# A list schedule's model of VectorE, GpSimd and TensorE: when one holds the other, how long GpSimd takes, how early TensorE may be planned

## The chip, the cores and the metric

One core of one Trainium2 chip runs the whole program. The metric is device microseconds of one execution. The kernel before takes 1219.08 us (median of three runs, 1217.67 to 1220.74).

Names in the profile: PE is TensorE (its weight loads are PEld), DVE is VectorE, ACT is ScalarE, POOL is GpSimd, SP is the engine that issues the DMAs.

## The reference

Attention with queries averaged in pairs, then a gated feed-forward block that mixes along the sequence. There are 8 batches and 8 heads; 1152 keys and 576 queries of width 64.

```python
q_pool = q.reshape(B, H, S // 2, 2, D).mean(axis=3)
scores = scale * np.matmul(q_pool, k.transpose(0, 1, 3, 2))
scores = scores - np.max(scores, axis=-1, keepdims=True)
attn = np.exp(scores)
attn = attn / (np.sum(attn, axis=-1, keepdims=True) + 1e-09)
x = np.matmul(attn, v)              # laid out as (8, 576, 512)
...
h = np.maximum(x @ w_in, 0.0)
u, v = (h[..., :d_ff // 2], h[..., d_ff // 2:])
v_n = (v - mu) / np.sqrt(var + 1e-06)
v_s = np.einsum('ts,bsd->btd', w_spatial, v_n) + b_spatial[None, :, None]
out = (u * v_s) @ w_out
```

All of it is kept near float32 by splitting each float32 operand into a float16 head and a float16 rest and multiplying the parts.

## The kernel before, in words

**Attention.** The two heads of a pair lie on the two halves of the partitions, so there are 32 pairs, `i` = 0 to 31. For each pair, `prep` squares, scales and splits the queries and keys (the part that VectorE does in the first eight pairs, by `rest`, L387, GpSimd does later, L605), and issues DMAs on SP that bring the parts into place. `maxima` multiplies queries and keys roughly (L641, tiles `pm` and `pw`: 27 products of 128x384 a pair), VectorE takes the largest of each product (L647, `mt`), and `shift` makes a row of it (L660 to L670), turned by TensorE (L668). While `units` holds a gated unit, `maxima` takes all its tiles from the two banks of `pm`; without one it alternates between these and the two of `pw`. `attention` then makes the exact scores in 18 steps of two matmuls (L842, L843, tile `pss`), ScalarE takes the exponent (L848, tile `pt`, eight buffers), GpSimd subtracts the upper half of each float32 from it and so leaves a float16 rest (L868, 128x512), and `values` multiplies with V in three groups of four matmuls: two on the upper halves (L745, L751), which need ScalarE alone, and one on the rests (L756), which needs GpSimd too. What is left over of the queries (64 of each head) goes through `ptl` in the same manner, with one GpSimd instruction of 128x1152 for each pair.

**The gated part.** Two batches make a unit, four units in all. `gated_unit` multiplies with w_in (L926, L990), normalises (L962 to L974 on VectorE and ScalarE), mixes along the sequence (L1031, L1032), gates (L1038, L1041), splits (L387, tile `vv`) and multiplies with w_out (L1074). Units 0 to 2 are fed in small pieces between the steps of attention; the last one runs behind the attention.

**What sets the order.** The program is written down once in the order of these generators. Then `Order.pin` makes a list schedule: it has a cost for each instruction (`cost`: how long the engine is taken, and when the result is there), keeps the time at which each engine is free, and again and again takes the earliest instruction that may start on any engine; on one engine the one that was written first goes first among those that are due. What it takes is chained to the engine's instruction before it, so the order on every engine is the plan's order, and on the chip only semaphores decide when each starts. An instruction is due when its producers are through, plus `DELAY`, plus `SLACK` for its pair of engines: with `("Pool", "PE")` at 2100 ns, a matmul that reads what GpSimd made is not due until 2.1 us after the planned end of that. The slack bears on the choice alone; the planned start of what is chosen leaves it out (`there`, not `due`).

`two_from_sbuf` marks instructions that may hold each other up: on VectorE tensor by tensor, tensor by scalar and copy with no operand in PSUM, and on GpSimd all of its tensor subtractions and additions. For these the plan keeps `held`, the start and end of the last planned GpSimd instruction, and `dve`, when the last such VectorE instruction lets GpSimd go:

```python
if e == "DVE":
    if t >= held[0]:
        t = max(t, held[1] - 130)
    dve = t + out
else:
    t = max(t, dve)
    held = (t, t + out)
```

So in the plan a VectorE instruction that starts at or after the start of a GpSimd one begins 130 ns before the end of it at the soonest, and a GpSimd instruction begins when the VectorE one has ended.

Of the kernel before, what the change touches and what calls it, by code (L numbers as in the profile page):

```python
# [10 lines left out]
F16 = mybir.dt.float16  # L11
BF16 = mybir.dt.bfloat16
F32 = mybir.dt.float32
# [18 lines left out]
class Order:  # L32

    LANES = ("PE", "Activation", "DVE", "Pool", "SP")
    DELAY = {("PE", "Activation"): 114, ("Activation", "Pool"): 77}
    SLACK = {("Pool", "PE"): 2100, ("Activation", "PE"): 300, ("DVE", "PE"): 300, ("SP", "PE"): 500}
    SIZE = {F16: 2, BF16: 2, F32: 4, I32: 4, U32: 4, I64: 8}

    def __init__(self):
# [106 lines left out]
    def cost(self, lane, ins):  # L148

        xs = [x.bass_ap for x in list(ins.ins) + list(ins.outs) if hasattr(x, "bass_ap")]  # L150
        count = lambda ap: math.prod([d[1] for d in ap.ap][1:])
        if lane == "PE":
            n = count(xs[0])
            t = max(28.5, n / 2.4 + 2.5)
            if xs[0].dtype == F32:
                t = 110 if n == 128 else max(224, 4 * n / 2.4)
            return t, t + 148
        if lane == "SP":
            big = max((count(x) * x.ap[0][1] * self.SIZE[x.dtype] for x in xs), default=0)
            return (1230 if "Transpose" in ins.opcode else 560), 2400 + big / (100 if "Transpose" in ins.opcode else 230)  # L160
        n = max((count(x) for x in xs), default=1)
        psum = any(self.slot.get(x.tensor.name, (0, 0))[1] for x in xs)

        flat = sum(count(x) == 1 for x in xs[:-1]) if n > 1 else 0
        wide = len(xs) - 1 - flat
        if lane == "Activation":
            t = 0.84 * n + (157 if psum else 188) + 85 * (min(flat, 2) or (n == 1 and wide > 1))
            if len(ins.outs) > 1:
                return t - 10, t + 95
            return t - 105, t  # L170
        elif lane == "DVE":
            plain = ins.opcode == "TensorScalarPtr"
            if plain and wide < 2 and not psum or ins.opcode == "TensorCopy":
                t = 0.55 * n + 140 + 60 * flat
            else:
                t = 1.04 * n + 145 + 65 * (flat > 0 and plain)
        else:
            t = {F32: 2.1, F16: 2.0, BF16: 1.74}[xs[1].dtype] * n + 150
            return t - 42, t
        return t - 84, t  # L180

# [5 lines left out]
    def pin(self, tc):  # L187
        names = {getattr(mybir.EngineType, e): e for e in self.LANES}
        fixed = ("RegisterMove", "TensorScalarAffineSelect", "Memset")
        prog = [i for i in tc.nc.cur_bb.bb.instructions if i.engine in names and i.opcode not in fixed]  # L190
        before, begun = self.edges(prog)
        loose = {i.name for a, z, skip in self.lined if skip for i in tc.nc.cur_bb.bb.instructions[a:z]}
        early = {i.name for i in tc.nc.cur_bb.bb.instructions[: self.seen]} - loose
        ahead = None
        for n, i in enumerate(prog):
            if names[i.engine] == "SP" and i.name not in loose:
                if ahead is not None and ahead not in before[n]:
                    begun[n].add(ahead)
                if i.name in early:
                    ahead = n  # L200
        after = [[] for _ in prog]
        left = []
        lane = [names[i.engine] for i in prog]
        for n, (pre, beg) in enumerate(zip(before, begun)):
            left.append(len(pre) + len(beg))
            for m in pre:
                after[m].append((n, True))
            for m in beg:
                after[m].append((n, False))
        cost = [self.cost(e, i) for e, i in zip(lane, prog)]  # L210
        shared = [e in ("DVE", "Pool") and self.two_from_sbuf(i) for e, i in zip(lane, prog)]
        held, dve = (0.0, 0.0), 0.0
        ready = {e: [n for n in range(len(prog)) if lane[n] == e and not left[n]] for e in self.LANES}
        due = [0.0] * len(prog)
        there = [0.0] * len(prog)
        free = dict.fromkeys(self.LANES, 0.0)
        wire = 0.0
        load = {n for n, i in enumerate(prog) if lane[n] == "SP" and i.ins and i.ins[0].bass_ap.tensor.name not in self.slot}
        last = {}
        dep = mybir.DependencyInfo(mybir.DependencyClass.NoSync, mybir.DependencyReason.DATA)  # L220
        for _ in prog:
            best = None
            for e, ns in ready.items():
                if ns:

                    at = {n: max(due[n], wire - 1000) if n in load else due[n] for n in ns}
                    if e == "DVE":
                        for n in ns:
                            if shared[n] and max(free[e], at[n]) >= held[0]:
                                at[n] = max(at[n], held[1] - 130)  # L230
                    t = max(free[e], min(at.values()))
                    n = min(n for n in ns if at[n] <= t)
                    if best is None or t < best[0]:
                        best = (t, e, n)
            t, e, n = best
            ready[e].remove(n)
            own, out = cost[n]
            t = max(free[e], there[n])
            if shared[n]:

                if e == "DVE":
                    if t >= held[0]:
                        t = max(t, held[1] - 130)
                    dve = t + out
                else:
                    t = max(t, dve)
                    held = (t, t + out)
            if e == "SP":
                wire = max(wire, t + own) + (out - 2400)
                end = wire + 1700  # L250
            else:
                end = t + out
            free[e] = t + own
            if e in last:
                tc.add_manual_dep(prog[n], last[e], dep, reason="order")
            last[e] = prog[n].name
            for m, through in after[n]:
                left[m] -= 1
                if not through:
                    x = t  # L260
                elif lane[m] != e:
                    x = end + self.DELAY.get((e, lane[m]), 52)
                else:
                    x = t if e == "PE" else end + 34
                there[m] = max(there[m], x)
                due[m] = max(due[m], x + (self.SLACK.get((e, lane[m]), 0) if through else 0))
                if not left[m]:
                    ready[lane[m]].append(m)
        self.span = max(free.values())
# [964 lines left out]
```

## Time and profile before

| | before |
|---|---|
| median of 3 runs | 1219.08 us |
| the profiled execution | 1220.91 us |
| its span in the trace | 1219.1 us |
| granted TensorE clock, mean | 0.987 |
| ACT busy | 890.8 us (73%) |
| HBM read, written | 81.20 MB, 9.44 MB |

The span is what the trace covers of the program's instructions; 1.8 us of the execution lie outside it. A view by windows gives, for each stretch of the span, how long each engine was busy in it and how many instructions that were. A view of waits tells which instruction's idle time was ended by which. In a timeline, a row is the start, the length, engine, line, operation, the tile written and the tiles read, and the shape; where equal instructions follow one another, they are merged and counted, and what stands in brackets is the engine's idle time before the row, and what ended it.

### The profile page before, as it was taken

Reading aid. Unit: us, or ns where it says so; the run is one execution under the profiler, and the core shown is the slowest. Engines: PE = TensorE matmul, PEld = TensorE weight load, DVE = VectorE, ACT = ScalarE, POOL = GpSimd, SP = SyncE. Lnnn points to the kernel's source line nnn. Section 1 sums busy time; section 2 is a strip of 40 time slices with the busy share of each in tenths; the row PEclk is TensorE's granted clock in tenths of the full one; section 3 lists DMA queues with packets and bytes.
Section 4 is the critical chain, followed back from the end, with each engine's and each line's share of the span. In section 5 each row is a group of like instructions: output and inputs, shape, how many; then the busy total and the mean of one; then the engine's idle time right before and its main releaser. Section 6 shows DMA issues by size and latency. Waiting matters only on the chain.

```text
span 1219.1 us, 33464 instructions
## 1 busy us (share of the span) xinstructions
PE 1160.2 (95%) x13296; PEld 726.5 (60%) x13296; DVE 887.9 (73%) x2228; ACT 890.8 (73%) x1675; POOL 841.1 (69%) x726
## 2 busy tenths in 40 slices
PE   3988999999998999999999999999999999999998
PEld 1656666766655666566665666566665666655453
DVE  5699989987889577766679676865669866841644
ACT  4887779789976877978777877878776876744433
POOL 2545657678886878888887887788887786874000
PEclk9889999999999999999999999999999999999999
DMA  5455455445432454255442443256334421211002
GB/s 190 163 156 161 123 178 143 125 119 153 130 87 77 138 123 123 73 158 152 114 101 75 125 140 82 65 143 204 99 98 103 103 70 49 48 47 45 1 1 79
DMA packets 88446, 132.97 MB, mean 109 GB/s; under 512 B 39840, under 2 KB 48032, under 8 KB 87776
## 3 DMA queue, kind: packets, MB, share of 16 engines
q1 hardware_dynamic: 88288, 130.82, 38.4%
q8 instruction: 104, 1.70, 0.6%
q14 instruction: 54, 0.44, 0.1%
HBM read 81.20 MB, written 9.44 MB: 74 GB/s over the span
## 4 chain that ended last, share of the span: by engine, by line
PE 71%; DVE 22%; issue 2%; ACT 1%; DMA 1%; POOL 0%; SPq 0%; DVEq 0%; ACTq 0%
DVE mt L647 8%; PE pss L842 7%; PE pss L843 7%; PE pm L641 7%; PE pw L1031 7%; PE pw L926 6%; PE pw L1074 5%; PE pw L990 5%; PE o L745 4%; PE o L756 4%; PE o L751 4%; DVE vv L387 2%; PE o L738 1%; DVE row L962 1%; PE pss L926 1%
## 5 line engine op out<-in xcount | busy, mean ns | idle before, releaser
L868 POOL TENSOR_TENSOR pt<-pt 128x512 f16<-128x512 f32 x528 | 574.1, 1103 | 195.8 <-ACT pt L848 193.0
L848 ACT ACTIVATE pt<-pss,esc 128x512 f32<-128x512 f32 x576 | 388.3, 689 | 140.4 <-PE pss L843 124.7
L647 DVE TENSOR_REDUCE mt<-pm 128x1 f32<-128x384 f32 x733 | 387.9, 551 | 102.3 <-PE pm L641 84.0
L842 PE MATMUL pss<-qhi,khi 128*128 128x512 f16 x576 | 220.9, 384 | 2.0 <-ACT pt L848 1.7
L843 PE MATMUL pss<-xq,klo 66*128 66x512 f16 x576 | 221.6, 386 | 0.0
L641 PE MATMUL pm<-khi,qhi 128*128 128x384 f16 x655 | 204.0, 329 | 17.7 <-DVE mt L647 12.6
L745 PEld LDWEIGHTS <-pt 128*128 128x128 bf16 x2112 | 119.3, 99 | 62.2 <-DVE xm L764 6.5
L745 PE MATMUL o<-vp,pt 128*128 128x65 f16 x2112 | 155.1, 193 | 0.7 <-DVE xm L764 0.4
L756 PE MATMUL o<-vp,pt 128*128 128x65 f16 x2112 | 154.1, 193 | 0.0
L751 PE MATMUL o<-vp,pt 128*128 128x64 f16 x2112 | 151.7, 193 | 0.0
L756 PEld LDWEIGHTS <-pt 128*128 128x128 f16 x2112 | 117.7, 98 | 49.5 <-issue 2.7
L641 PEld LDWEIGHTS <-qhi 128*128 128x128 f16 x768 | 74.1, 100 | 70.7 <-issue 28.2
L751 PEld LDWEIGHTS <-pt 128*128 128x128 bf16 x2112 | 101.1, 98 | 3.2 <-issue 0.7
L868 POOL TENSOR_TENSOR ptl<-ptl 128x1152 f16<-128x1152 f32 x32 | 71.7, 2241 | 26.4 <-ACT ptl L864 26.3
L926 PE MATMUL pw<-wi_h,xg 128*128 128x512 f16 x240 | 89.1, 379 | 0.0
L647 DVE TENSOR_REDUCE mt<-pw 128x1 f32<-128x384 f32 x131 | 69.8, 546 | 16.2 <-PE pw L641 16.0
L864 ACT ACTIVATE ptl<-pss,esc 128x256 f32<-128x256 f32 (+1 forms) x128 | 64.0, 500 | 23.5 <-PE pss L859 22.6
L990 PE MATMUL pw<-xg,wi_h 128*128 128x512 f16 (+1 forms) x336 | 80.7, 325 | 0.0
L1074 PE MATMUL pw<-wo_h,vv 128*128 128x512 f16 x216 | 80.1, 379 | 0.6 <-DVE vv L387 0.4
L1031 PE MATMUL pw<-ws_h,vv 128*128 128x512 f16 x216 | 80.2, 379 | 0.0
L843 PEld LDWEIGHTS <-klo 66*128 66x128 f16 x576 | 56.6, 98 | 35.7 <-issue 10.4
L842 PEld LDWEIGHTS <-khi 128*128 128x128 f16 x576 | 56.7, 98 | 27.0 <-issue 6.0
(204 smaller groups left out, 2520.7 us busy)
## 6 DMA issues: line engine op xcount, KB each, us to landing
vt<-in_v_dram SPq DMA_DIRECT2D x56, 576.0 KB
qt<-in_qT_dram SPq DMA_DIRECT2D x32, 576.0 KB
kt<-in_kT_dram SPq DMA_DIRECT2D x32, 576.0 KB
khi<-kn SPq DMA_DIRECT2D x128, 144.0 KB
out_dram<-row SPq DMA_DIRECT2D x24, 256.0 KB
qhi<-xq SPq DMA_DIRECT2D x64, 72.0 KB
klo<-klo SPq DMA_DIRECT2D x32, 144.0 KB
vv<-in_w_in_dram SPq DMA_DIRECT2D x4, 1024.0 KB
```

Of the source, the lines that this page charges most:

```text
L641: nc.tensor.matmul(pm[:, :W], lhsT=qhl[:, h, c0 : c0 + P], rhs=khh[:, h, n * NB : (n + 1) * NB, :], start=True, stop=True,)
L647: nc.vector.reduce_max(out=mt[:, t, n : n + 1], in_=pm[:, :W], axis=AX.X)
L745: nc.tensor.matmul(o[:, t], lhsT=top[:, cols], rhs=vp[:, D : D + D1], start=c == 0 and t == 0, stop=False, skip_group_check=True,)
L751: nc.tensor.matmul(o[:, t, 0:D], lhsT=top[:, cols], rhs=vp[:, 0:D], start=False, stop=False, skip_group_check=True)
L756: nc.tensor.matmul(o[:, t], lhsT=rst[:, cols], rhs=vp[:, D : D + D1], start=False, stop=c == NC - 1, skip_group_check=True,)
L842: nc.tensor.matmul(o, lhsT=khh[:, h, c, :], rhs=qhl[:, h, q], start=True, stop=False)
L843: nc.tensor.matmul(o, lhsT=KL[0:KR, h, c, :], rhs=X[0:KR, h, q], start=False, stop=True)
L848: nc.scalar.activation(pt, ps, AF.Exp, bias=0.0, scale=esc)
L868: nc.gpsimd.tensor_sub(t.bitcast(F16)[..., 0::2], t, t.bitcast(BF16)[..., 1::2])
L926: nc.tensor.matmul(ph, lhsT=xa[:, cc, c0 : c0 + P], rhs=wa[:, cc, DH:DF], start=n == 0, stop=n == 3 * NCC - 1,)
L990: nc.tensor.matmul(pu[:, : z - a], lhsT=wa[:, cc, fc * P : (fc + 1) * P], rhs=xa[:, cc, a:z], start=n == 0, stop=n == 3 * NCC - 1,)
L1031: nc.tensor.matmul(pv, lhsT=l, rhs=r[:, 0:MAIN], **fl)
```

## The change

No instruction is added, taken away or altered. The plan's model differs in these places, and with it, possibly, the order on each engine:

- **The start margin, `GRAB` = 85 ns.** A marked VectorE instruction that would start less than 85 ns before a GpSimd one counts as held by it, too; and when the plan asks which engine's next event comes first, such a VectorE instruction is entered 85 ns later than its start.
- **The ends of a hold.** A held VectorE instruction begins 175 ns (was 130) before the end of the GpSimd one. A GpSimd instruction may begin 139 ns before the end of the VectorE one (was at its end).
- **Lengths on GpSimd**, by the type of its second input, for n elements a partition: 2.17 n + 150 for float32 (was 2.1 n + 150), 1.91 n + 175 for float16 (was 2.0 n + 150), 1.67 n + 185 for bfloat16 (was 1.74 n + 150). On ScalarE instructions with an operand in PSUM are 5 ns longer.
- **Slack ahead of TensorE**: 1400 ns after GpSimd (was 2100), 400 after VectorE (was 300), 1000 after SP (was 500), 300 after ScalarE as before.

```diff
+    GRAB = 85
+    SLACK = {("Pool", "PE"): 1400, ("Activation", "PE"): 300, ("DVE", "PE"): 400, ("SP", "PE"): 1000}
-    SLACK = {("Pool", "PE"): 2100, ("Activation", "PE"): 300, ("DVE", "PE"): 300, ("SP", "PE"): 500}
...
-            t = 0.84 * n + (157 if psum else 188) + 85 * (min(flat, 2) or (n == 1 and wide > 1))
+            t = 0.84 * n + (162 if psum else 188) + 85 * (min(flat, 2) or (n == 1 and wide > 1))
...
-            t = {F32: 2.1, F16: 2.0, BF16: 1.74}[xs[1].dtype] * n + 150
+            t = {F32: 2.17 * n + 150, F16: 1.91 * n + 175, BF16: 1.67 * n + 185}[xs[1].dtype]
...
-                            if shared[n] and max(free[e], at[n]) >= held[0]:
-                                at[n] = max(at[n], held[1] - 130)
+                            if shared[n] and max(free[e], at[n]) + self.GRAB >= held[0]:
+                                at[n] = max(at[n], held[1] - 175)
...
-                    if best is None or t < best[0]:
-                        best = (t, e, n)
-            t, e, n = best
+                    key = t + self.GRAB * (e == "DVE" and shared[n])
+                    if best is None or key < best[0]:
+                        best = (key, e, n, t)
+            _, e, n, t = best
...
-            if shared[n]:
-
-                if e == "DVE":
-                    if t >= held[0]:
-                        t = max(t, held[1] - 130)
-                    dve = t + out
-                else:
-                    t = max(t, dve)
-                    held = (t, t + out)
+            if e == "Pool":
+                t = max(t, dve)
+                held = (t, t + out)
+            elif shared[n]:
+                if t + self.GRAB >= held[0]:
+                    t = max(t, held[1] - 175)
+                dve = t + out - 139
```

## The prediction

> **What bounds the kernel now.** I read the page's busy times first, then the busy times by stage, then the waits.
>
> ```profile
> span 1219.1 us, 33464 instructions
> PE 1160.2 (95%) x13296; PEld 726.5 (60%) x13296; DVE 887.9 (73%) x2228; ACT 890.8 (73%) x1675; POOL 841.1 (69%) x726
> ```
>
> ```profile
> 0.00:60.00 60.00, 38.90 (x312) 22.74 (x313) 35.79 (x93) 37.71 (x77) 24.39 (x30) 0.86 0.54 179
> 60.00:240.00 180.00, 162.89 (x1895) 116.11 (x1895) 173.56 (x390) 144.88 (x270) 109.52 (x83) 0.96 0.49 146
> 240.00:400.00 160.00, 152.55 (x1811) 97.52 (x1810) 134.01 (x330) 129.02 (x246) 124.35 (x105) 1.00 0.41 113
> 400.00:1100.00 700.00, 690.67 (x8469) 431.12 (x8467) 492.05 (x1291) 533.74 (x1001) 570.52 (x499) 1.00 0.40 106
> 1100.00:1219.10 119.10, 115.24 (x819) 58.98 (x817) 52.51 (x127) 45.50 (x84) 12.30 (x12) 1.00 0.09 30
> ```
>
> The columns behind the length are PE, PEld, DVE, ACT, POOL, and then the granted clock. TensorE is the bound: it idles 58.9 us of the span, 21.1 of them in the first 60 us, 17.1 from 60 to 240, 7.5 from 240 to 400, 9.3 from 400 to 1100 and 3.9 at the end. From 60 to 240 VectorE is nearly full as well (173.56 of 180). A schedule that does the same matmuls can win only out of this idle time; the 33.9 us from 60 to 1100 are what this change can reach, since the start is loads and the end is the last unit, where GpSimd does nothing. Who ends TensorE's waits in these 33.9 us (matmuls first, then the weight loads that share their sequencer):
>
> ```profile
> PE pm L641 <- DVE mt L647: 11.2, 21, 1.2
> PE pw L668 <- DVE mc L664: 5.7, 6, 2.1
> PE pw L641 <- DVE mt L647: 4.5, 5, 2.0
> PE pm L641 <- DVE xt L820: 3.2, 5, 1.1
> PE pm L668 <- DVE mc L664: 1.6, 6, 0.5
> PE pss L842 <- ACT pt L848: 1.3, 3, 0.9
> PE pm L632 <- DVE mt L647: 1.3, 1, 1.3
> ```
>
> ```profile
> PEld L668 <- DVE mc L664: 15.1, 21, 2.2
> ```
>
> Six of the seven rows of matmuls, 27.5 us in 44 waits, are VectorE being late. GpSimd and DMA do not appear. So the question is how late VectorE comes, and whether the plan knew it.
>
> **The hold, the first part of the change.** What VectorE and GpSimd do to each other can be read from single instructions. One uncontended split of 128x576 at the end, where GpSimd is silent, and the same operation in mid-run:
>
> ```profile
> L387 DVE SCALAR_TENSOR_TENSOR xg<-u,gs,xg 128x576 f16<-128x576 f32 x8 | 6.2, 814 | 3.7 <-ACT xg L384 3.7
> L387 DVE SCALAR_TENSOR_TENSOR vv<-u,gs,vv 128x576 f16<-128x576 f32 x24 | 26.5, 1137 | 0.0
> L387 DVE SCALAR_TENSOR_TENSOR qhi<-qt,qks,xq 128x576 f16<-128x576 f32 x32 | 33.0, 1031 | 2.4 <-ACT xq L384 2.4
> ```
>
> These two groups alone lose 24 x (1137 - 814) + 32 x (1031 - 814) = 7.8 + 6.9 = 14.7 us to holds. Now single cases, GpSimd's row first:
>
> ```profile
> 490.69 3.04 POOL L868 TENSOR_TENSOR pt<-pt 128x512 f16<-128x512 f32 x3
> ```
>
> ```profile
> 492.66 1.69 DVE L387 SCALAR_TENSOR_TENSOR vv<-u,gs,vv 128x576 f16<-128x576 f32 x1
> ```
>
> ```profile
> 888.95 2.60 POOL L868 TENSOR_TENSOR pt<-pt 128x512 f16<-128x512 f32 x2
> ```
>
> ```profile
> 888.83 0.81 DVE L387 SCALAR_TENSOR_TENSOR qhi<-qt,qks,xq 128x576 f16<-128x576 f32 x1
> ```
>
> ```profile
> L868 POOL TENSOR_TENSOR pt<-pt x528: 1032/1043/2066, 33.3 to 1115.1; 128x512 f16<-128x512 f32 x176
> L868 POOL TENSOR_TENSOR ptl<-ptl x32: 2106/2111/2654, 41.4 to 1095.7; 128x1152 f16<-128x1152 f32 x32
> L566 POOL TENSOR_TENSOR qt<-qt x32: 1394/1404/2076, 5.5 to 981.1; 128x576 f32<-128x576 f32 x32
> L550 POOL TENSOR_TENSOR vp<-vt,vp x48: 1226/1237/1407, 269.3 to 1068.8; 128x576 f16<-128x576 f32 x48
> ```
>
> In the first case three back-to-back subtractions of about 1.04 us run from 490.69 to 493.73, so the third begins near 492.69, some 0.03 us after the split began at 492.66. The split loses all the same: it ends at 494.35, which is 493.73 + 0.62, as if it had begun 0.19 before GpSimd's end. In the second GpSimd begins 0.12 after the split; now the split takes its 0.81, and GpSimd pays: two subtractions take 2.60 instead of 2 x 1.04, so they begin 0.52 late, at 889.47 to 889.50, which is 0.14 to 0.17 before the split's end at 889.64. So the margin lies between 0.03 and 0.12 (the change: 0.085), the end of a hold near 0.19 (130 ns before, 175 after) and GpSimd's release near 0.14 (0 before, 139 after). The three new constants are nearer to the trace than the old ones.
>
> The Trainium skill, "SBUF — State Buffer", says of this pair of ports that the engine that starts first has it for the whole instruction and the other fully blocks (section "Who interferes with whom"). The case at 492.66 speaks against reading that as the order of the starts. By that rule the margin would be wrong; what this would make of the time is a rival below.
>
> In cases of the first kind the old plan lets VectorE go first and GpSimd wait. The trace has eight in which a marked instruction began 0 to 90 ns before GpSimd's and was held; the first and the last:
>
> ```profile
> 329.30 1.66 DVE L387 SCALAR_TENSOR_TENSOR ws_l<-u,wss,ws_h 128x576 f16<-128x576 f32 x1
> ```
>
> ```profile
> 1065.18 2.75 DVE L387 SCALAR_TENSOR_TENSOR vv<-u,gs,vv 128x576 f16<-128x576 f32 x1
> ```
>
> Against 0.81 they lose 0.85 and 1.94, and the eight 7.9 us. With the margin the plan sees these and puts a maximum (from PSUM, not marked) ahead. How much TensorE feels: behind the case at 1065.18 it waited 1.27 us, two thirds of the 1.94:
>
> ```profile
> 1068.45 0.32 PE L632 MATMUL pm<-kn,qd 128*128 128x384 f16 x1 [1.27 <-DVE mt L647]
> ```
>
>  VectorE has room in these stages (492.05 of 700), so less elsewhere. Bounds 0 and 7.9 gained (a loss here is the first rival); I take a little under half, **-3.5 us**. Queued behind a marked instruction that is put off are the rest of the unit's splits and the matmuls L1074 that wait for them; they have other work of TensorE beside them.
>
> **VectorE's slack, 300 to 400.** The 44 waits above are late arrivals. Planned 100 ns later, each shrinks by at most 0.1 if TensorE has other work: 4.4 us at most. From 60 to 240 VectorE is the limit, and shuffling matmuls wins nothing. The waits for VectorE behind that are about 27:
>
> ```profile
> PE pm L641 <- DVE mt L647: 8.0, 15, 1.2
> PEld L668 <- DVE mc L664: 8.0, 14, 1.2
> ```
>
> (240 to 1060; with the matmuls of L668 and the rows for L820, 27 in the matmul rows.) 27 x 0.1 = 2.7; I take **-2.5**, bounds 0 and -4.4, unless the bank turns slow (rival).
>
> **Lengths.** By the formulas the plan had 2154 ns for `ptl` and has 2109 (trace 2111), for `qt` 1360 and 1400 (1404), for `vp` 1302 and 1275 (1237), for `pt` 1041 and 1040 (1043). These are under 50 ns against a slack of more than 1000, so they act only through the holds. 45 ns of `ptl` in each of 32 pairs is 1.4 us and the others partly cancel; bounds 0 and 2 gained, I take **-1**. ScalarE's 5 ns: nothing, ScalarE is 73% busy.
>
> **GpSimd's slack, 2100 to 1400.** The matmuls on the rests (L756) come 0.7 us sooner in the plan. The margin in the trace, from GpSimd's end to the first L756 that reads it, has a median of 3.1 us and is under 0.7 in six of 528. The tightest and its neighbour:
>
> ```profile
> 766.68 3.06 POOL L868 TENSOR_TENSOR pt<-pt 128x512 f16<-128x512 f32 x3
> ```
>
> ```profile
> 769.14 0.28 PE L756 MATMUL o<-vp,pt 128*128 128x65 f16 x4
> ```
>
> The second of the three ends near 768.74, so its margin is 0.40, and 0.30 is missing if the matmul moves up by 0.7. The six lack 0.9 together. TensorE takes its queue in order: while it waits there, scores, maxima and the unit's matmuls stand behind. I take **+1**, bounds 0 and 4 (were GpSimd 1 us later in a dozen places). What the earlier matmuls give, `pt` buffers that come free sooner, helps ScalarE, which is not late (1.3 us in the waits).
>
> **SP's slack, 500 to 1000.** No DMA ends a wait of TensorE's from 60 to 1100. The cover is the three-set depth of the keys and queries; without it, each pair's first maxima would stop. **0**, bounds -1 and +1 in the first 60 us.
>
> **Sum.** -3.5 - 2.5 - 1 + 1 = -6 us. The profiled execution took 1220.91 us, 1.8 more than the median of 1219.08, so it becomes 1214.9, and the median **1213.1 us**. All gains at their bounds, -7.9 - 4.4 - 2, give 1204.8.
>
> **The rivals.**
>
> *The holds only change places.* The plan drifts from the chip, so a margin of 85 ns at one place is a collision at another. For: most of the loss (14.7 us in two groups alone against 7.9 in eight cases) is holds that the old plan could foresee, with GpSimd long at work, and VectorE had nothing else to do or the plan was off by more than 0.1. Against: six of the eight cases lie in the units' splits and normalisations, which come round with every unit in the same phase. Time: the gains go, and the +1 stays or not: 1217 to 1221.
>
> *The bank's round trip (slower).* While a unit is pending, the maxima have two banks. In the plan one round is 162 ns of matmul + 148 + 52 + 544 of VectorE's maximum + 52 + slack = 1258 before and 1358 after, so back-to-back maxima come every 629 ns before and 679 after, 50 ns more each. For: VectorE already waits for these products:
>
> ```profile
> DVE mt L647 <- PE pm L641: 84.0, 156, 4.7
> ```
>
> ```profile
> L647 DVE TENSOR_REDUCE mt<-pm 128x1 f32<-128x384 f32 x524 | 276.8, 552 | 91.7 <-PE pm L641 76.5 <-PE pm L632 7.8 <-PE pm L360 2.5
> ```
>
> 524 maxima from 400 to 1100 are 26 us. Against: VectorE is free for 208 us of that stage. It decides where VectorE has less than 27 x 0.05 = 1.35 us free in a pair, the starts and ends of units. If half of the 26 reaches TensorE: 1219.1 - 6 + 13 = 1226.
>
> *Start order decides.* By the reading of the ports that the row at 492.66 denies, the margin would put VectorE off without need: its 3.5 go, 1216.6.
>
> *It does nothing.* If no choice in the plan changed, 1219.1. With 700 ns less slack ahead of each of 528 groups of matmuls that is unlikely.
>
> **How the numbers follow.** Forecast (faster) 0.54; holds change places 0.22; the bank 0.19; start order 0.03; nothing 0.02. A measurement can tell some 0.3% from no change, 3.7 us: faster is below 1215.4, slower above 1222.7. The two small rivals and the first count as the same: 0.54, 0.27, 0.19. The forecast's own range is 1204.8 to 1215.4. The range runs from 1204 to 1224: below it I leave 0.05, above it some 0.14, most of the bank's case.
>
> **What would show it.** Right: the mean of the 24 splits of `vv` under 1137; TensorE busy above 152.55 and 690.67 in stages no longer than before; the waits of L641 and L668 for VectorE smaller in sum, the typical one by 0.1; margins of L756 some 0.7 smaller in the median, with a wait for GpSimd below 1 us in sum. Wrong: the same holds at other instructions; VectorE's idle ahead of L647 well above 91.7 us from 400 to 1100 with TensorE waiting for it (the bank); TensorE waiting for L868 by several us.

## The result, and the profile after

The changed kernel takes 1198.0 us (median of four runs, 1197.3 to 1198.87) against 1219.71 for the kernel before (1217.67 to 1220.74, four runs): a ratio of 0.9824 with a 95% interval of 0.9807 to 0.9841, 21.7 us faster. Forecast were 1213.1 us and a range from 1204; the sign was right and the size was not. The profiled execution took 1198.15 us, with a span of 1196.4.

The page of the changed kernel, busy times:

```profile
span 1196.4 us, 33475 instructions
PE 1152.7 (96%) x13296; PEld 726.0 (61%) x13296; DVE 867.3 (72%) x2228; ACT 889.3 (74%) x1675; POOL 844.0 (71%) x726
```

VectorE ran the same 2228 instructions in 867.3 us instead of 887.9, 20.6 us less, and its holds (summed below) account for it. TensorE idles 43.7 us instead of 58.9, and is busy 7.5 us less with the same 13296 matmuls. By stage (PE, PEld, DVE, ACT, POOL, the granted clock):

```profile
0.00:60.00 60.00, 39.30 (x330) 23.63 (x331) 38.13 (x95) 38.34 (x78) 24.55 (x30) 0.86 0.54 179
60.00:240.00 180.00, 166.35 (x1990) 119.69 (x1987) 172.84 (x405) 150.34 (x281) 113.48 (x88) 0.98 0.52 153
240.00:400.00 160.00, 158.41 (x1899) 101.80 (x1899) 128.88 (x341) 136.17 (x263) 135.56 (x113) 1.00 0.45 123
400.00:1100.00 700.00, 696.10 (x8522) 435.96 (x8521) 478.68 (x1276) 529.42 (x987) 570.36 (x496) 1.00 0.38 104
```

From 60 to 240 TensorE got 1990 matmuls done instead of 1895, and 1899 instead of 1811 in the next stage. Where the time went is told better by the same events than by the same windows, since the kernels drift apart. The first product of each gated unit (L926) starts at

| | unit 0 | unit 1 | unit 2 | unit 3 | end |
|---|---|---|---|---|---|
| before | 277.7 | 562.4 | 843.7 | 1117.4 | 1219.1 |
| after | 268.3 | 547.8 | 824.7 | 1094.7 | 1196.4 |
| gained so far | 9.4 | 14.6 | 19.0 | 22.7 | 22.7 |

So 9.4 us come from the stage before the first unit, where VectorE is full, then 4 to 5 with each unit, and nothing from the last unit, which GpSimd does not share. TensorE's waits from 60 to 1100 us, after:

```profile
PE pw L641 <- DVE mt L647: 5.9, 8, 2.1
PE pm L641 <- DVE mt L647: 1.9, 6, 0.7
PE pm L641 <- DVE xt L820: 1.5, 2, 1.2
PE pw L668 <- DVE mc L664: 1.5, 2, 1.1
```

```profile
PEld L668 <- DVE mc L664: 5.4, 10, 1.2
```

The two rows of `pm` and `pw` behind `mt` went from 15.7 us in 26 waits to 7.8 in 14, L668's weight loads from 15.1 to 5.4. The groups on VectorE, first the one row of before that is not shown yet, then after:

```profile
L962 DVE TENSOR_SCALAR row<-vv,mv,rs 128x512 f32<-128x512 f32 x36 | 28.0, 793 | 0.2
```

```profile
L647 DVE TENSOR_REDUCE mt<-pm 128x1 f32<-128x384 f32 x733 | 388.1, 551 | 105.2 <-PE pm L641 87.0 <-PE pm L632 13.7 <-PE pm L360 1.2
L387 DVE SCALAR_TENSOR_TENSOR qhi<-qt,qks,xq 128x576 f16<-128x576 f32 x32 | 30.8, 963 | 1.2 <-ACT xq L384 1.1
L387 DVE SCALAR_TENSOR_TENSOR vv<-u,gs,vv 128x576 f16<-128x576 f32 x24 | 26.2, 1103 | 0.0
L962 DVE TENSOR_SCALAR row<-vv,mv,rs 128x512 f32<-128x512 f32 x36 | 20.5, 585 | 0.3
```

The largest single fall is L962, the normalisation, 36 x (793 - 585) = 7.5 us. The splits `vv`, which the prediction leaned on, hardly moved (a mean of 1103 ns after 1137).

Two sums are used below. **Held** is the time that marked VectorE instructions took beyond the uncontended time of their kind (instructions over it by 60 ns or more): 60.5 us in 89 instructions before, 37.8 in 72 after. **Unknown** is the part of it that the plan did not have: since the plan's order is the chip's order, each instruction of the trace can be laid beside its planned one, and those count that are held at least 100 ns longer than planned. That is 51.8 us in 76 instructions before and 20.7 in 36 after. The plan's own sum of holds is 19.2 us before and 32.7 after: the new plan has more of them, the chip fewer. Along the five stretches between the events of the table above, held time fell by some 10, 5, 5, 4 and 0 us, where the time gained is 9.4, 5.2, 4.4, 3.7 and 0.0.

### The profile page after: what moved, and what is told of

It reads as the page before. It is cut to its first block, busy times and chain, and to the rows that moved or that the text cites. A ratio compares the mean times of both kernels' runs of the same rounds, so it can differ in the third digit from the quotient of the medians.

```text
span 1196.4 us, 33475 instructions
## 1 busy us (share of the span) xinstructions
PE 1152.7 (96%) x13296; PEld 726.0 (61%) x13296; DVE 867.3 (72%) x2228; ACT 889.3 (74%) x1675; POOL 844.0 (71%) x726
## 4 chain that ended last, share of the span: by engine, by line
PE 79%; DVE 15%; ACT 2%; issue 1%; DMA 0%; DVEq 0%; ACTq 0%
PE pss L842 9%; PE pss L843 8%; PE pm L641 7%; DVE mt L647 7%; PE pw L1031 7%; PE pw L926 6%; PE pw L1074 6%; PE pw L990 6%; PE o L745 5%; PE o L756 4%; PE o L751 4%; PE o L738 2%; PE pss L926 1%; PE pss L1031 1%; PE pss L1074 1%; PE pss L855 1%
## 5 line engine op out<-in xcount | busy, mean ns | idle before, releaser
L647 DVE TENSOR_REDUCE mt<-pm 128x1 f32<-128x384 f32 x733 | 388.1, 551 | 105.2 <-PE pm L641 87.0
L745 PEld LDWEIGHTS <-pt 128*128 128x128 bf16 x2112 | 123.9, 98 | 69.2 <-DVE xm L764 3.5
L756 PE MATMUL o<-vp,pt 128*128 128x65 f16 x2112 | 155.4, 193 | 0.0
L751 PE MATMUL o<-vp,pt 128*128 128x64 f16 x2112 | 154.4, 193 | 0.0
L756 PEld LDWEIGHTS <-pt 128*128 128x128 f16 x2112 | 114.1, 98 | 35.3 <-issue 0.8
L751 PEld LDWEIGHTS <-pt 128*128 128x128 bf16 x2112 | 102.0, 98 | 3.0
L926 PE MATMUL pw<-wi_h,xg 128*128 128x512 f16 x240 | 89.3, 379 | 0.0
L864 ACT ACTIVATE ptl<-pss,esc 128x256 f32<-128x256 f32 (+1 forms) x128 | 63.8, 499 | 22.6 <-PE pss L859 22.3
L647 DVE TENSOR_REDUCE mt<-pw 128x1 f32<-128x384 f32 x131 | 70.2, 548 | 14.2 <-PE pw L641 13.8
L566 POOL TENSOR_TENSOR qt<-qt 128x576 f32<-128x576 f32 x32 | 47.2, 1474 | 35.7 <-DMA qt<-in_qT_dram 32.5
```

Source lines behind the costliest of these rows:

```text
L647: nc.vector.reduce_max(out=mt[:, t, n : n + 1], in_=pm[:, :W], axis=AX.X)
L745: nc.tensor.matmul(o[:, t], lhsT=top[:, cols], rhs=vp[:, D : D + D1], start=c == 0 and t == 0, stop=False, skip_group_check=True,)
L751: nc.tensor.matmul(o[:, t, 0:D], lhsT=top[:, cols], rhs=vp[:, 0:D], start=False, stop=False, skip_group_check=True)
L756: nc.tensor.matmul(o[:, t], lhsT=rst[:, cols], rhs=vp[:, D : D + D1], start=False, stop=c == NC - 1, skip_group_check=True,)
L926: nc.tensor.matmul(ph, lhsT=xa[:, cc, c0 : c0 + P], rhs=wa[:, cc, DH:DF], start=n == 0, stop=n == 3 * NCC - 1,)
```

## The experiments

All twenty kernels in one table: the median, its ratio to the kernel before on the same chip, then from the profile VectorE's busy time, held and unknown, and for how long TensorE's clock was granted at half rate between 40 and 1150 us of the span. All in us but the ratio.

| kernel | us | ratio (95%) | DVE busy | held | unknown | half clock |
|---|---|---|---|---|---|---|
| before | 1219.7 | | 887.9 | 60.5 | 51.8 | 16.1 |
| after | 1198.0 | 0.9824 (0.9807-0.9841) | 867.3 | 37.8 | 20.7 | 8.4 |
| hold_alone | 1205.4 | 0.9881 (0.9866-0.9895) | 865.4 | 36.7 | 20.5 | 19.2 |
| slack_alone | 1222.5 | 1.0019 (0.9995-1.0044) | 891.7 | 63.8 | 55.3 | 14.6 |
| lengths_alone | 1214.5 | 0.9951 (0.9936-0.9966) | 880.6 | 54.9 | 46.1 | 23.2 |
| no_slack | 1198.0 | 0.9823 (0.9804-0.9842) | 860.9 | 34.2 | 15.4 | 23.3 |
| margin_alone | 1202.5 | 0.9864 (0.9846-0.9883) | 871.5 | 43.0 | 24.9 | 12.9 |
| ends_alone | 1206.5 | 0.9894 (0.9875-0.9914) | 874.4 | 47.3 | 35.4 | 12.7 |
| lengths_mirrored | 1205.9 | 0.9890 (0.9868-0.9911) | 872.0 | 44.5 | 36.1 | 16.7 |
| hold_mirrored | 1218.9 | 0.9993 (0.9975-1.0011) | 884.5 | 58.6 | 51.6 | 16.1 |
| before_nudge_a | 1215.1 | 0.9960 (0.9947-0.9974) | 886.6 | 59.2 | 50.5 | 8.8 |
| before_nudge_b | 1215.6 | 0.9962 (0.9941-0.9983) | 880.5 | 54.8 | 45.6 | 31.2 |
| after_nudge | 1197.5 | 0.9819 (0.9788-0.9849) | 863.1 | 33.5 | 17.9 | 8.2 |
| no_hold_in_plan | 1234.0 | 1.0115 (1.0083-1.0147) | 885.1 | 60.1 | 60.1 | 22.0 |
| after_margin_0 | 1204.2 | 0.9880 (0.9842-0.9917) | 871.7 | 45.2 | 33.9 | 14.4 |
| after_margin_170 | 1196.2 | 0.9807 (0.9782-0.9832) | 861.8 | 34.2 | 29.9 | 9.9 |
| after_margin_300 | 1203.2 | 0.9856 (0.9825-0.9888) | 864.7 | 36.0 | 32.2 | 25.5 |
| after_margin_600 | 1201.3 | 0.9846 (0.9819-0.9872) | 864.1 | 34.8 | 28.5 | 19.0 |
| before_short_max | 1208.0 | 0.9899 (0.9884-0.9914) | 860.3 | 51.0 | 44.6 | 8.2 |
| after_short_max | 1189.7 | 0.9752 (0.9736-0.9768) | 841.5 | 29.7 | 12.0 | 8.1 |

### The parts of the change

The first theory was the prediction's: the hold is the main part. The rivals were that the slack is, or that any new order of the plan scatters by as much, whatever it means.

`hold_alone` is before with the new scheduling loop:

```diff
+    GRAB = 85
-                            if shared[n] and max(free[e], at[n]) >= held[0]:
-                                at[n] = max(at[n], held[1] - 130)
+                            if shared[n] and max(free[e], at[n]) + self.GRAB >= held[0]:
+                                at[n] = max(at[n], held[1] - 175)
...
+                dve = t + out - 139
```

> The kernel before with the change's new rules for the hold alone (the margin of 85 ns, 175 ns, 139 ns); lengths and slack as before. The change as a whole gained 21.5 us. Theory 1, the hold is the main part as the prediction ranked it (3.5 of 7 us of gains): 10 to 13 us faster, 1207 to 1210. Theory 2, the slack is the main part: 0 to 5 us faster. Theory 3, any other order of the plan scatters by several us whatever its meaning: between 6 faster and 6 slower, and the parts will not add up to 21.5.

`slack_alone`:

```diff
-    SLACK = {("Pool", "PE"): 2100, ("Activation", "PE"): 300, ("DVE", "PE"): 300, ("SP", "PE"): 500}
+    SLACK = {("Pool", "PE"): 1400, ("Activation", "PE"): 300, ("DVE", "PE"): 400, ("SP", "PE"): 1000}
```

> The kernel before with the four new slacks alone. Theory 1 (hold): 4 to 8 us faster, since 44 waits of TensorE for VectorE shrink by at most 0.1 us each. Theory 2 (slack): 14 us faster or more, 1205 or less. Theory 3 (scatter): anything within 6 us of 1219.

`lengths_alone`:

```diff
-            t = 0.84 * n + (157 if psum else 188) + 85 * (min(flat, 2) or (n == 1 and wide > 1))
+            t = 0.84 * n + (162 if psum else 188) + 85 * (min(flat, 2) or (n == 1 and wide > 1))
...
-            t = {F32: 2.1, F16: 2.0, BF16: 1.74}[xs[1].dtype] * n + 150
+            t = {F32: 2.17 * n + 150, F16: 1.91 * n + 175, BF16: 1.67 * n + 185}[xs[1].dtype]
```

> The kernel before with GpSimd's new lengths and ScalarE's 5 ns alone. Theories 1 and 2: 0 to 2 us faster, since no length moves by more than 45 ns. Theory 3 (scatter): as far from 1219 as the other two, up to 6 us to either side.

`no_slack` is the changed kernel with the old line of slacks:

> The changed kernel with the old slacks: hold and lengths together. Theory 1: 12 to 15 us faster than before. Theory 2: 1 to 6 us faster. Theory 3: not the sum of what hold and lengths give alone; off from it by 4 us or more.

Measured: the hold alone 14.5 us faster, the slack alone nothing (its ten runs spread from 1216 to 1231, with the mean granted clock from 0.989 down to 0.973), the lengths alone 5 to 6 faster, hold and lengths without the slack 1197.96, the same as the whole change. The four slacks are worth nothing here, with the old hold or with the new. What TensorE waited for from 60 to 1100 us under the new slacks alone:

```profile
PE pm L641 <- DVE mt L647: 8.6, 12, 1.6
PE pw L668 <- DVE mc L664: 5.3, 4, 2.2
PE pw L641 <- DVE mt L647: 4.5, 4, 2.1
```

There are fewer waits (12 and 4 behind `mt`, against 21 and 5), but those left are longer, and their sum fell by 2.6 us only, without making the run shorter. What went are short waits; the long ones, late maxima, stayed.

### Is it the trace's constants, or any others?

`margin_alone` has the 85 ns in the test and in the choice, with 130 and 0 kept; `ends_alone` has 175 and 139 and `GRAB = 0`. The mirrored kernels move the constants of before as far the other way, away from the trace:

```diff
-            t = {F32: 2.1, F16: 2.0, BF16: 1.74}[xs[1].dtype] * n + 150
+            t = {F32: 2.03 * n + 150, F16: 2.09 * n + 125, BF16: 1.81 * n + 115}[xs[1].dtype]
...
```

```diff
...
-                        t = max(t, held[1] - 130)
-                    dve = t + out
+                        t = max(t, held[1] - 85)
+                    dve = t + out + 139
```

> The kernel before with the margin of 85 ns alone (the test and the entry in the choice); a hold still ends at 130 and 0. The three rules together gained 14.5 us. If the margin is the main part, as the prediction had it: 8 to 14 us faster, and the holds in which GpSimd began 0 to 90 ns after VectorE fall from eight to a few. If it is the ends of the hold: 0 to 4 faster. If any new order scatters: within 6 of 1219 to either side.

> The hold's new rules with the margin at 0: only 175 for 130, and GpSimd released 139 ns before VectorE's end. If the margin is the main part: 0 to 4 us faster. If the ends are: 8 to 14 faster, since in the old plan each GpSimd instruction behind a marked one is 139 ns late, some 90 times in a run, and the plan drifts from the chip. Scatter: within 6 of 1219.

> The kernel before with the lengths moved by as much the other way (2.03, 2.09, 1.81 ns an element with 150, 125, 115; ScalarE 5 ns shorter), so farther from the trace. The new lengths alone gained 6 us. If nearness to the trace is what counts: 2 to 8 us slower. If any new order scatters about 1219, or the old one is an unlucky one: as likely faster, up to 6.

> The kernel before with the ends of the hold moved the other way: a held VectorE instruction begins 85 ns before GpSimd's end (130), and GpSimd waits 139 ns past VectorE's end (0); no margin. Nearness to the trace: 3 to 12 us slower, with more held time on VectorE. Scatter: within 6 of 1219 to either side.

The margin alone gave 17.3 us and the ends alone 13.4, against 14.5 for both: they do not add, either one gives about as much as both. And the lengths moved away from the trace gave 13.9 us, more than those moved towards it. So "nearer to the chip, hence faster" fails for the lengths; they act as a nudge of the order, and a new order that means nothing can thus be worth as much as 13.9 us here. For the ends of the hold the mirror gained nothing.

A finding against the prediction's reason for the margin: the held cases in which GpSimd began 0 to 90 ns after VectorE, eight before, are eight again with the margin alone, and that kernel is 17 us faster (the changed kernel has three). Nor does one margin tell who is held. In the kernel before, sixteen marked instructions of 0.5 us or more began 0 to 85 ns ahead of a GpSimd one. Eight of them are the held ones; the other eight kept their own time. Two of those, with leads of 0.06 and 0.01 us, each with GpSimd's row behind it:

```profile
189.59 0.80 DVE L387 SCALAR_TENSOR_TENSOR vp<-vt,vs,vp 128x576 f16<-128x576 f32 x1
```

```profile
189.65 2.01 POOL L566 TENSOR_TENSOR qt<-qt 128x576 f32<-128x576 f32 x1
```

```profile
915.74 0.69 DVE L968 TENSOR_TENSOR vv<-row,vv 128x512 f16<-128x512 f32 x1
```

```profile
915.75 1.70 POOL L775 TENSOR_TENSOR xc<-xm,xc 128x512 f16<-128x512 f32 x1
```

Here GpSimd pays: the medians of L566 and L775 are 1.40 and 1.16 us. So "VectorE is held when it leads by less than 85 ns" was right in eight of sixteen cases. What else decides is open.

### How much is luck?

With theory 1 (the margin wins by near misses) shaken and theory 3 (scatter) in part borne out, a fourth was formed: what costs is held time that the plan did not know, since the maxima behind it come late for matmuls that the plan has put there. It goes with most of the times so far: 51.8 us unknown at 1219.7, 20.7 at 1198.0, 35.4 and 36.1 at 1206; `hold_alone`, with 20.5 at 1205.4, does not fit as well.

The nudges change one number of the plan by 1 ns: the latency of a matmul's result (148 to 149, `before_nudge_a` and `after_nudge`), or the delay between engines (52 to 53, `before_nudge_b`). `no_hold_in_plan` takes the hold out of the plan:

```diff
-        shared = [e in ("DVE", "Pool") and self.two_from_sbuf(i) for e, i in zip(lane, prog)]
+        shared = [False] * len(prog)
```

> The kernel before with one meaningless nudge: the plan has every matmul's result 149 ns after its own time (148). Theory 4, surprise: what counts is the held time of VectorE that the plan did not know (60.5 us held in the trace against 19.2 in the plan's own sum for before, 37.8 against 32.7 after); a nudge leaves it about 40, so 1213 to 1222. Theory 3, the order before was unlucky: any nudge gives 1203 to 1212, as the mirrored lengths did with 1206.

> The kernel before with another nudge: the plan's delay between engines is 53 ns (52). Theory 4 (surprise): 1210 to 1222, and wherever it lands the held time in the trace less the plan's goes with it, some 0.5 us of time for 1 us. Theory 3 (unlucky): 1203 to 1212.

> The changed kernel with the first nudge (149 for 148). Theory 4 (surprise): the plan still knows the hold, 1194 to 1203. Theory 3 (luck): the changed kernel was a lucky draw out of a scatter about 1208, so 1203 to 1212.

> The kernel before with no hold in the plan at all: no instruction is marked, so the plan counts 0 us of held time. Theory 4 (surprise): VectorE's held time in the trace is 60 us or more, all of it unknown, 1222 to 1235. Theory 3 (scatter): within 6 of 1208 to 1219, no worse than before.

The nudged kernels before came out at 1215.1 and 1215.6, the nudged changed kernel at 1197.5. So a nudge of 1 ns is worth up to 5 us, and the nudged kernels stay on their own sides. The seven kernels with neither the margin nor the new ends (before, its nudges, the slack, the two with other lengths, the mirrored hold) have a mean of 1216.0 (1205.9 to 1222.5); the eight with a margin have 1200.3 (1196.2 to 1205.4); the two with the new ends and no margin 1205.3. By these means about 16 of the 21.7 us belong to the rule, and that figure is itself good to a few microseconds only: the groups touch at their ends, and their kernels were not drawn at random. Held time separates them more cleanly: every kernel in the table with a margin has 43.0 us or less of it, every one without 44.5 or more, though the gap is narrow. The rest of the 21.7 is luck: the order before was one of the slower of its group and the changed one a better one of its own.

Without any hold in the plan the kernel takes 1234 us. Its page:

```profile
span 1232.2 us, 33496 instructions
PE 1165.1 (95%) x13296; PEld 728.4 (59%) x13296; DVE 885.1 (72%) x2228; ACT 893.9 (73%) x1675; POOL 840.5 (68%) x726
```

VectorE is busy as long as before (885.1 and 887.9) and held as long (60.1 and 60.5). What differs is that none of it was planned, 5.9 us more at half clock, and TensorE's waits behind it:

```profile
PE pm L641 <- DVE mt L647: 17.7, 23, 2.3
PE pm L632 <- DVE mt L647: 5.2, 4, 1.7
```

The same row of `pm` behind `mt` was 11.2 in 21 waits before and is 1.9 in 6 after. That speaks for theory 4, but it is one kernel, and orders scatter by as much.

### Is a narrow lead what costs?

Laid beside the plan of before, 51 of the 76 unknown holds have the plan start VectorE less than 300 ns ahead of the time at which GpSimd was ready, or after it. If so, a margin wider than 85 ns should win more. The changed kernel with `GRAB` at 0, 170, 300 and 600:

> The changed kernel with the margin at 0 instead of 85 ns. Theory 4a, narrow leads: the plan again lets VectorE go first by a few ns, held time it does not know rises from 20.7 to 35 us or so, 1203 to 1212. Theory 4b, nearness to the chip: slower too, by the eight cases alone, 1198 to 1204.

> The changed kernel with the margin at 170 ns, twice what the chip shows. Theory 4a (narrow leads): unknown held time falls below 15 us and the time by 2 to 6 us, 1192 to 1196. Theory 4b (nearness to the chip): a margin that the chip does not have puts VectorE off for nothing, 1198 to 1206.

> The changed kernel with the margin at 300 ns. Theory 4a (narrow leads): as good as 170 or better, 1188 to 1196, with less than 10 us unknown. Theory 4b: worse than 170, 1200 to 1212.

> The changed kernel with the margin at 600 ns: VectorE's marked work only where GpSimd is free for a long time. The plan's own span is 7 us longer than with 85. Theory 4a: no more to win, and marked work comes late: 1194 to 1206, with the least held time of all. Theory 4b: 1205 to 1220.

Measured: 1204.2, then 1198.0 with 85, 1196.2, 1203.2, 1201.3. No margin costs some 6 us, as both theories had it; 170 is level with 85 (the intervals overlap); wider margins win nothing. Held time does not fall below 34 us, at 170 or at 600. The 6 us are hardly more than a nudge gives, so the narrow lead may be a part of it; that a wider one would win more is refuted. Theory 4 loses here too: with 170 ns the unknown part is 29.9 us instead of 20.7 (the plan's own sum of holds is 11.2) and the time is no longer. Held time as a whole, 34.2 and 37.8, goes with the time better than its unknown part. That 300 and 600 ns are slower is no more held time either (36.0 and 34.8): they have 25.5 and 19.0 us at half clock, against 8.4 and 9.9 for 85 and 170 (see the last section). With 300 ns the one run at a granted clock of 0.987 took 1198.7, those at 0.983 took 1203.8 and 1204.5.

### The order kept, VectorE's time cut elsewhere

Everything so far compares orders with orders. To see whether VectorE's time is itself what is paid for, two kernels keep every engine's order exactly. The maximum leaves out the last 24 of each product's 384 columns, and the plan goes on counting 384:

```diff
-                nc.vector.reduce_max(out=mt[:, t, n : n + 1], in_=pm[:, :W], axis=AX.X)
+                nc.vector.reduce_max(out=mt[:, t, n : n + 1], in_=pm[:, : W - 24], axis=AX.X)
...
-        n = max((count(x) for x in xs), default=1)
+        n = max((count(x) for x in xs), default=1); n = 384 if n == 360 else n
```

> The kernel before, every engine's order unchanged (the plan still counts 384), but each of the 864 maxima L647 reads 360 of its 384 columns; the kernel leaves the last 24 columns of each product out of the maximum. At 1.04 ns a column in the plan this is 25 ns each, 21.6 us less of VectorE's time, about what the change saved in holds (22.7). If VectorE's time is what TensorE pays for: 10 to 18 us faster, 1202 to 1210. If held time only goes along with some other quality of the order: 0 to 4 us faster.

> The changed kernel, order unchanged, with the same shorter maxima (the last 24 columns of each product left out). If VectorE's time is what is paid for, less is left to win than in before, since TensorE waits less for it: 5 to 12 us faster than the changed kernel, 1186 to 1193. If not: 1195 to 1199.

The page of `before_short_max`, and the maxima among its groups:

```profile
span 1205.6 us, 33470 instructions
PE 1155.1 (96%) x13296; PEld 724.6 (60%) x13296; DVE 860.3 (71%) x2228; ACT 889.8 (74%) x1675; POOL 843.6 (70%) x726
```

```profile
L647 DVE TENSOR_REDUCE mt<-pm 128x1 f32<-128x360 f32 x733 | 370.7, 526 | 113.5 <-PE pm L641 93.3 <-PE pm L632 11.6 <-PE pm L360 2.7
```

A maximum takes 25 ns less, and VectorE's busy time falls by 27.6 us (the maxima and, since they end sooner, some of the holds). With the same order the run is 12.5 us faster than before: 0.45 us for each us of VectorE. On the changed kernel, 25.8 us less give 8.3 us, 0.32 for each. The difference between the two is the clock: the first also lost half-clock time, 16.1 to 8.2 us, the second did not (8.4 and 8.1). Taken at the same granted clock, both come to 0.31 (last section). So VectorE's time is paid for directly, at about a third, when it is cut evenly from all maxima. By that price the 20.6 us that the change took off VectorE are worth some 6.4, and some 3.4 of the 21.7 went with the clock. The other 12 or so came through the new order: where the holds lie and what is planned around them. These were not separated further; a hold that makes one maximum late may well cost more than the same time spread over all of them, but no run here changed a hold alone. So it is not excluded that the orders with a margin are better in some other way too. The shortened kernels do less of the work and are no version to use; of the complete ones none is clearly ahead of the changed kernel.

## Why the prediction was wrong

**Right.** The sign, and where the time lay: VectorE late behind holds that the plan did not have, and the plan's new rules for the hold as the largest part. TensorE is the bound; its waits for VectorE shrank. The bank's round trip did not come: VectorE's idle ahead of L647 is 105.2 us after and was 102.3 in all, and from 400 to 1100 us 89.5 after 91.7. The median margin of L756 fell by 0.65 us (3.14 to 2.49), three of 528 are under 0.7, and TensorE waits for no GpSimd instruction. That no DMA ends a wait of TensorE's from 60 to 1100 is so but for two weight loads, 0.5 us in sum before; nothing rests on it.

**The step that failed** is the size of the hold: "the eight 7.9 us ... Bounds 0 and 7.9 gained", with -3.5 taken. It measured 14.5 alone and some 16 by the groups' means. The prediction saw 14.7 us of holds in two groups, and put all but the eight cases down as "holds that the old plan could foresee, with GpSimd long at work". That GpSimd is long at work in the trace does not say that the plan had it so. Laid side by side, 76 of the 89 holds were unknown to the old plan, 51.8 us of 60.5. The bound of 7.9 came from the eight cases alone; it should have come from all the held time that the plan did not have. And the margin does not act by the eight cases (eight again with the margin alone, at 1202.5). The reading behind it, a margin between 0.03 and 0.12 from two single cases, does not hold for the trace either: eight of sixteen VectorE instructions with a lead under 85 ns were not held. How the margin lowers held time stays open. Shown is that it does: all nine kernels with a margin have less held time (29.7 to 43.0 us) than any of the eleven without (44.5 to 63.8).

**From 60 to 240 nothing to win from matmuls.** The sentence was meant for the slack, but the sum has nothing else for this stage. 9.4 us were gained by the start of the first unit, while held time fell by some 10 us there, in a stage where VectorE is full, and the time at half clock from 60 us on fell by 6.8.

**The slack for VectorE, -2.5; GpSimd's, +1.** Both together 0, from `slack_alone` and `no_slack`. The waits behind `mt` that are left under the new slacks have means of 0.7 and 1.1 us, and 100 ns does not cover that.

**The lengths, -1.** They measured -5 to -6 alone, but the mirrored ones measured -13.9 and a nudge of 1 ns up to -5, so nothing of it can be put down to their being right.

**What was not in the sum at all:** the scatter of the order itself, up to 5 us for a nudge and 13.9 for the mirrored lengths, and the clock (below), which made up part of it. The premise that the same matmuls leave only TensorE's idle time to win was wrong as well: of the 22.7 us of span, 15.2 came from idle time and 7.5 from busy time. 7.7 us less at half rate would account for about half of the 7.5; the rest is not explained here. The range's lower end, 1204.8 from three bounds, could not hold all this.

**The rivals.** That the holds only change places is refuted (60.5 to 37.8 us). That the order of the starts decides: the row at 492.66 and seven like it speak against it, while the eight that were not held agree with it; the 6 us that a margin of 0 costs are too near a nudge to settle it. What the Trainium skill says in "SBUF — State Buffer" ("Who interferes with whom"), that whoever issues first has the ports, speaks of the issue, not of the start as the prediction put it. It may still hold; the start in the trace, as at 492.66 (0.04 us ahead, and held), is not that order.

## What to carry to other kernels

When a list schedule decides the order, lay its plan beside the trace instruction by instruction, and sum the waits that the plan did not have. Here that sum, 51.8 us, would have warned that 7.9 us of near misses was too small a bound. Nudge one constant by 1 ns on both versions before believing a gain of a few microseconds, and mirror the constants before believing that they won because they are right. Compare runs at the same granted clock as well: part of a gain, and most of what the first nudge gave, can be the clock.

## What the runs showed of the hardware

**The clock turns waits into longer waits.** From 60 to 240 us the view by windows gives 0.96 before and 0.98 after. It is not a slow drift: the clock is granted at half rate in whole stretches, 6.8 us from 66.3 and then, in the kernel before, two more of 3.4 us. Stretches of before, each first the 3.4 us ahead and then the one at half clock (the granted clock is the third number from the end):

```profile
158.50:161.90 3.40, 1.35 (x19) 0.97 (x20) 3.40 (x7) 0.98 (x3) 2.62 (x3) 1.00 0.35 141
161.90:165.30 3.40, 3.40 (x29) 2.81 (x29) 1.75 (x6) 3.18 (x6) 0.00 (x0) 0.50 0.19 20
230.20:233.60 3.40, 1.90 (x9) 0.67 (x7) 3.40 (x6) 3.40 (x7) 3.40 (x3) 1.00 0.13 29
233.60:237.00 3.40, 3.26 (x33) 2.89 (x32) 2.55 (x6) 2.06 (x4) 3.38 (x4) 0.50 0.37 66
```

The wait ahead of the first one is VectorE's again:

```profile
160.55 0.22 PE L668 MATMUL pw<-ident_h,mc 128*8 128x128 f16 x1 [2.12 <-DVE mc L664]
```

TensorE was busy 1.35 and 1.90 us of the 3.4 ahead, 0.40 and 0.56 of it, and then ran 3.4 us at half clock. The changed kernel has neither. Its half-clock time from 60 to 1150 us is one stretch of 6.8 us from 65.5, against 6.8 + 3.4 + 3.4 before. In the traces of the twenty kernels the stretches from 60 to 1150 us are 3.4 us or a multiple.

A fit of the spans of the first eighteen kernels of the table gives 0.79 us for each us of held time and 0.49 for each us at half clock; all but the kernel without a hold in its plan (11.6 us above the fit) lie within 4.5 us of it. For before and after it gives 22.7 x 0.79 + 7.7 x 0.49 = 21.7 of the 22.7 us between the spans. But that is a fit over different orders, and its 0.79 is not a price: VectorE's time cut in a kept order gave 0.31.

The repeated runs show the clock with the order kept. The kernel before ran 59 times beside the experiments, and its granted clock was not the same each time: three runs at 0.983 took 1223.3 us in the mean, six at 0.990 took 1216.3. That is 7.0 us with one and the same program, for an estimated 2 x 0.007 x 1220 = 17 us at half clock, 0.41 us for each. At 0.990 the changed kernel takes 1198.0, so the change is worth 18.3 of its 21.7 us at an equal clock. `before_short_max` takes 1207.8 there and `after_short_max` 1190.0: 8.5 / 27.6 and 8.0 / 25.8, 0.31 both times. `before_nudge_a` takes 1215.0, so 1.3 of its 5.1 us are left. (Each of these is a mean of two to six runs, on different chips.)

The Trainium skill, "TensorE: Matmul & The Clock Gate" (Part 1), has two states, half and full, and a window of about 3.4 us, and the traces agree: the rows above have 0.50 and 1.00, in stretches of 3.4 us. Its table has the fall to half after one idle window or more. Here windows were enough in which TensorE was busy 0.40 and 0.56 of the time.
